# Block 2's norm and inverse by chunk halves, norms of blocks 3 and 4 queued behind queries, attention one step earlier

## Chip, core and metric

The kernel runs on one core of one Trainium2 chip. The metric is device time in microseconds (us). Before the change it is 1829.39 us (median of 3 runs, 1828.8 to 1829.55).

## What is computed

A gated linear recurrence over 768 steps for 4 sequences, 8 heads and 48 channels, and behind it a mixture of 8 experts whose gate is normalised over rows and columns eight times:

```
a = (a_re + i a_im) * min(|a|, 0.999) / (|a| + 1e-6)
S[t] = a[t] * S[t-1] + k[t] v[t]^T          # complex state, per head 48 x 48
y[t] = q[t] . Re S[t]
x = y as [3072, 384];  P = exp(x @ w_gate - max);  8 times: P /= row sums, P /= column sums, P *= 3072/8
out = sum over e of P[:, e] * (relu(x @ w1[e]) @ w2[e])     # w1: 384 x 1024, w2: 1024 x 384
```

## The kernel before, in words

The 3072 tokens are cut into 12 blocks of 256, each of two chunks of 128; a sequence has three blocks. Phase 1 works through the blocks; at the same time it runs experts 0 and 1 on the block before. Phase 2 runs the other six experts and the gate's iterations.

**Per block, VectorE and ScalarE** (`elem`, `chain`, L361 and L422). The decays `z` of the block are loaded. Then come the **norm** (L435 to L449: a square on ScalarE, a reciprocal root on ScalarE, two corrections, seven VectorE instructions that end with two products `z<-z,x`), the **scan** (L451: cumulative complex products inside each chunk of 128, some 45 small VectorE instructions), and the **inverse** (L457 to L472: square, reciprocal root and one correction, then the scaled keys `kh`, L470, and the queries `z<-z,qk`, L472). The names `sqs[i, n]` and `zl[i, n]` are the last ScalarE and the last VectorE instruction of the inverse of block i, half n. With `parts=None` each step is one instruction over both chunks (768 elements a partition); with `range(NCH)` it is one for each chunk (384). Before the change blocks 0 and 1 go by halves.

**Per block, attention** (`mix`, L475). Twelve DMAs on SyncE's queue (L495) move `kh` into `ks`, twelve on GpSimd's queue move `z` into `qs`, six for each chunk. Then TensorE transposes the keys (`ktp`, L516), forms scores (`sp`, L533) and state products (`U`, L526) and outputs (`y`, L550). VectorE masks the scores (`sc`, L536) and moves the state (L587 to L598). `mix` is a generator that is advanced ten times a block; the first advance issues keys and scores of chunk 0.

**Per block, experts** (`experts`, L176). Sixteen steps on the block before, two experts of eight slices. A step is nine matmuls into `ph` (L214), two ScalarE readings `hh` and `hf` (L226, L227), one VectorE difference `hl` (L228), and, three steps later, six matmuls into `po` (L187 to L189), the third of which needs `hl`. When an expert ends, `po` is copied to `yst` (L192) and stored to `ye_d` by SyncE's queue (L193).

**Order.** TensorE's order is written out by hand: step n of block i's loop, then one advance of `mix` if n is at least `LEAD[i]` (L330). What is left of `mix` after step 15 alternates with the last expert matmuls. The other engines' orders come from a scheduler that goes by priority (order of emission) on a simulated timeline; `issue_after(ins)` puts what a block of code emits behind `ins` on the engine of `ins`, and `add_manual_dep` does so for one pair. Each engine and each DMA queue then works strictly in its order. In block 1's loop the expert steps 7 to 9 are held behind instructions of the inverse of block 1 (`late`, L316).

Of the kernel before, what the change touches and what calls it, by code (L numbers as in the profile page):

```python
# [23 lines left out]
N1 = 8  # L24
RING = 12
LAG = 3
LEAD = {1: 12, 2: 11, 3: 10, 4: 7, 5: 5}
TR = 4
TB = 32
UN = 768  # L30
# [30 lines left out]
class Net:  # L61
# [9 lines left out]
    def build(self):  # L71
        tc, nc = self.tc, self.nc
        DR = bass.MemoryType.DRAM
        PS = bass.MemoryType.PSUM
        with ExitStack() as ctx:
            dram = ctx.enter_context(tc.tile_pool(name="dram", bufs=1, space=DR))
            cst = ctx.enter_context(tc.tile_pool(name="cst", bufs=1))
            self.wp = ctx.enter_context(tc.tile_pool(name="wp", bufs=RING))
            self.psA = ctx.enter_context(tc.tile_pool(name="psA", bufs=2, space=PS))

            self.ones = cst.tile([128, 128], F32, name="ones")
            nc.vector.memset(self.ones, 1.0)
            warm = cst.tile([128, 1], F32, name="warm")
            nc.scalar.activation(warm, self.ones[:, 0:1], AF.Abs_reciprocal_sqrt)
            self.ident = cst.tile([128, 128], F32, name="ident")
            nc.sync.dma_start(self.ident, self.idn)
            self.nident = cst.tile([128, 128], F32R, name="nident")
            nc.scalar.activation(self.nident, self.ident, AF.Copy, scale=-1.0)
            self.mask = cst.tile([128, 4, CH], U8, name="mask")
            tri = cst.tile([128, CH], F32, name="tri")  # L90
            nc.sync.dma_start(tri, self.msk)
            for j in range(4):
                nc.vector.tensor_copy(self.mask[:, j, :], tri)
            self.bm05 = cst.tile([128, 1], F32, name="bm05")
            nc.vector.memset(self.bm05, -0.5)
            self.wgs = cst.tile([128, NCT, 2 * E], F32R, name="wgs")
            self.two = cst.tile([2 * E, E], F32, name="two")
            nc.vector.tensor_tensor(self.two, self.ident[:2 * E, :E], self.ident[:2 * E, E:2 * E], ALU.add)
            wgr = cst.tile([128, NCT, E], F32, name="wgr")
            nc.sync.dma_start(wgr, self.wg)  # L100
            nc.scalar.activation(self.wgs[:, :, :E], wgr, AF.Copy)
            nc.vector.tensor_tensor(self.wgs[:, :, E:], wgr, self.wgs[:, :, :E].bitcast(F32), ALU.subtract)
            self.P = cst.tile([128, self.ntt, E], F32, name="P")

            ns = self.N // SUB
            self.fl = cst.tile([128, ns * (NCT * NCH + 2) + 4], F32, name="fl")
            self.ok = cst.tile([128, 9], F32, name="ok")
            self.oki = cst.tile([1, 1], mybir.dt.int32, name="oki")
            self.wt = {}
            self.x_d = [dram.tile([128, NS, 2, NCT, 2, CH], F32, name=f"x_d{u}") for u in range(self.N // UN)]  # L110
            self.ye_d = [[dram.tile([128, C], F32, name=f"ye_d{u}_{i}") for i in range(self.ntt)] for u in range(2)]
            self.dram = dram

            with ExitStack() as c2, tc.manual_schedule(engines={mybir.EngineType.PE}):
                with ExitStack() as c1:
                    with ExitStack() as ca:
                        self.phase1(c1, ca)
                    self.phase2a(c2)
                self.phase2b(c2)
            flag = nc.values_load(self.oki[0:1, 0:1], min_val=0, max_val=1)  # L120
            with tc.If(flag < 1):
                with ExitStack() as c3:
                    self.general(c3)
# [52 lines left out]
    def experts(self):  # L176
# [18 lines left out]
        while True:  # L195
            i, e, f = yield
            if i is None:
                for _ in range(len(pend) if e is None else min(e, len(pend))):
                    l2(*pend.pop(0))
                continue  # L200
            if len(pend) == LAG:
                l2(*pend.pop(0))
            xh, xl = self.xs[i]

            def group(f):
                w = self.wt[e, f]
                ph = self.psA.tile([128, SUB], F32, tag="ph", name=f"ph{e}_{i}_{f}")
                terms = [(ct, k, x) for ct in range(NCT) for k, x in ((0, xh), (0, xl), (1, xh))]
                if e == 0 and f < 2:
                    terms.sort(key=lambda t: t[2] is xl)  # L210
                for q, (ct, k, x) in enumerate(terms):
                    if x is xl and terms[q - 1][2] is xh:
                        yield ph
                    nc.tensor.matmul(ph, w[:, k, ct * 128:ct * 128 + 128], x[:, ct, :], start=q == 0, stop=q == len(terms) - 1)  # L214
                yield ph

            if e == 0 and f == 0:
                rest = [group(0), group(1)]
                for g in rest:
                    next(g)  # L220
            for ph in rest.pop(0) if rest else group(f):
                pass
            hh = self.hp.tile([128, SUB], F32R, tag="hh", name=f"hh{e}_{i}_{f}")
            hl = self.hp.tile([128, SUB], F32R, tag="hl", name=f"hl{e}_{i}_{f}")
            hf = self.hp.tile([128, SUB], F32, tag="hf", name=f"hf{e}_{i}_{f}", bufs=2)
            nc.scalar.activation(hh, ph, AF.Relu)  # L226
            self.hf = nc.scalar.activation(hf, ph, AF.Relu)  # L227
            nc.vector.tensor_tensor(hl, hf, hh.bitcast(F32), ALU.subtract)  # L228
            pend.append((i, e, f, hh, hl))

    def phase1(self, c1, ca):
# [27 lines left out]
        for t in self.rr + [self.sb]:  # L259
            nc.gpsimd.memset(t, 0.0)  # L260
        self.xs, self.vt, self.kqd, self.ql, self.sqs, self.zl, self.post = {}, {}, {}, {}, {}, {}, {}
        self.ev, self.dve, self.act, self.root, self.nthird = [], {}, {}, {}, 0
        ns = self.N // SUB
        self.moe = self.experts()
        next(self.moe)
# [13 lines left out]
        for i in range(ns):  # L279
# [33 lines left out]
            lg = self.logits(i - 1)  # L313
            if i == 1:
                q, z = [self.sqs[1, n] for n in range(NCH)], [self.zl[1, n] for n in range(NCH)]
                late = {7: (q[0], z[0]), 8: (q[1], z[0]), 9: (z[1],)}  # L316
            for n in range(2 * NF):
                with ExitStack() as st:
                    if i == 1 and n in late:
                        for ins in late[n]:  # L320
                            st.enter_context(tc.issue_after(ins.ins))
                    self.moe.send((i - 1, n // NF, n % NF))
# [11 lines left out]
                    self.moe.send((None, 1, None))  # L334
            if i + 1 < ns:
                self.elem(i + 1)
        lg = self.logits(ns - 1)
        for f in range(2):
            self.moe.send((ns - 1, 0, f))
# [21 lines left out]
    def elem(self, i, scratch=False):  # L361
# [17 lines left out]
        if not scratch:  # L379
# [5 lines left out]
                nc.sync.dma_start(qk, self.aqk[i, :, 2:4])  # L385
            nc.sync.dma_start(vt, self.v[i])

            self.chain(i, range(NCH) if i == 1 else None, zt, qk, alloc)
            return

        for n in range(NCH):
# [30 lines left out]
    def chain(self, i, parts, zt, qk, alloc):  # L422
# [3 lines left out]
        base = 2 * ns + ns * NCT * NCH  # L426
        z = zt[:, :, :, :CH]
        sq, x, y0, zz = alloc("sq"), alloc("x"), alloc("y0"), alloc("zz")
        for n in parts or [None]:
            f0, f1 = (base + i, base + 2 + i) if n else (i, ns + i)  # L430
            sq_, x_, y_, zz_, z_ = (t if n is None else half(t, n) for t in (sq, x, y0, zz, z))
            with ExitStack() as st:
                if i == 2:
                    st.enter_context(tc.issue_after(self.sqs[1, 1].ins))
                act = self.act[i, n or 0] = [nc.scalar.activation(sq_, z_, AF.Square, accum_out=fl[:, f0:f0 + 1])]  # L435
            ops = self.dve[i, f"n{n or 0}"] = []
            with ExitStack() as st:
                if i == 2:
                    st.enter_context(tc.issue_after(self.zl[1, 1].ins))
                ops.append(V.scalar_tensor_tensor(x_, sq_[:, 0], 1e-20, sq_[:, 1], ALU.max, ALU.add))  # L440
            act.append(nc.scalar.activation(y_, x_, AF.Abs_reciprocal_sqrt))
            act.append(nc.scalar.activation(zz_, y_, AF.Square, accum_out=fl[:, f1:f1 + 1]))
# [12 lines left out]
        for n in parts or [None]:  # L455
            sq_, x_, g_, z_, qk_, kh_ = (t if n is None else half(t, n) for t in (sq, x, g0, z, qk, kh))
            act = nc.scalar.activation(sq_, z_, AF.Square)  # L457
            self.post.setdefault(i, []).append(act)
            V.scalar_tensor_tensor(x_, sq_[:, 0], 1e-26, sq_[:, 1], ALU.max, ALU.add)
            o = 2 * ns + i * NCT * NCH + (n or 0) * NCT  # L460
            self.root[i, n or 0] = [nc.scalar.activation(g_, x_, AF.Abs_reciprocal_sqrt)]
            nc.scalar.activation(fl[:, o:o + x_.shape[1]], x_[:, :, CH - 1], AF.Copy)
# [172 lines left out]
    def check(self, sp, more=lambda k: None):  # L635
# [2 lines left out]
        t = sp.tile([128, max(P.shape[1], fl.shape[1])], F32, name="chk")  # L638
        for j, (src, thr, op) in enumerate((
                (fl[:, 0:ns], 2.0 ** 40, ALU.is_le), (fl[:, ns:2 * ns], 2.0 ** 18, ALU.is_le),  # L640
                (fl[:, 2 * ns:-4], 1e-24, ALU.is_ge), (fl[:, -4:-2], 2.0 ** 40, ALU.is_le), (fl[:, -2:], 2.0 ** 18, ALU.is_le), (P, 3e38, ALU.is_le), (P, -3e38, ALU.is_ge))):
            o = t[:, :src.shape[1]]
            nc.vector.tensor_scalar(o, src, thr, None, op)
            nc.vector.tensor_reduce(ok[:, j:j + 1], o, AX.X, ALU.min)
# [458 lines left out]
```

## Time and profile before

| | |
|---|---|
| median of 3 runs | 1829.39 us |
| profiled execution, its own time | 1823.66 us |
| its span | 1821.5 us |
| TensorE busy | 1764.9 us, 97% |
| VectorE busy | 1359.3 us, 75% |
| ScalarE busy | 729.3 us, 40% |
| mean granted TensorE clock | 0.994 |

Busy time is what the profiler recorded on an engine; idle time of TensorE is time in which its next matmul waited. The columns of the rows further down are named with them. Blocks are numbered from 0; the loop of block 2, which the change touches most, lies between 116 and 175 us, and phase 1 ends near 600 us.

### The profile page before, as it was taken

How to read it: one execution, taken by the hardware profiler on the slowest of the kernel's cores; microseconds unless marked ns; L12 is line 12 of the kernel's file. 1: busy time of each engine (PE TensorE's matmuls, PEld its weight loads, DVE VectorE, ACT ScalarE, POOL GpSimd, SP SyncE). 2: the span in 40 equal slices, each digit the busy share in tenths (PEclk: the TensorE clock that was granted, in tenths of full speed). 3: DMA queues.
4: the chain of work that ended last, by engine and by line, in shares of the span. 5: the costliest groups of instructions: out<-in, count | busy, mean ns of one | idle time of the engine just before them, and what ended most of it. 6: DMA issues, size and time to landing. Idle time of an engine off the chain costs nothing.

```text
span 1821.5 us, 30688 instructions
## 1 busy us (share of the span) xinstructions
PE 1764.9 (97%) x12024; PEld 1724.2 (95%) x12024; DVE 1359.3 (75%) x3023; ACT 729.3 (40%) x1597; POOL 89.2 (5%) x168
## 2 busy tenths in 40 slices
PE   6997999999999999999999999999999999999998
PEld 3896999999999999899999999999999999999998
DVE  8889899888873587867576757687776767675754
ACT  7453444544543433333242424243433334342421
POOL 4101111111110000000000000000000000000000
PEclk9998999999999999999999999999999999999999
DMA  7424344433332421401020101232220101020100
GB/s 222 117 82 126 90 120 116 131 106 111 116 99 97 133 87 41 134 14 56 1 70 1 53 18 53 70 104 70 87 70 18 53 18 53 2 69 1 53 27 28
DMA packets 104504, 132.83 MB, mean 73 GB/s; under 512 B 9632, under 2 KB 82080, under 8 KB 104352
## 3 DMA queue, kind: packets, MB, share of 16 engines
q1 hardware_dynamic: 98944, 120.89, 21.8%
q0 software_dynamic: 4608, 9.52, 2.1%
q8 instruction: 96, 1.57, 0.4%
q14 instruction: 56, 0.46, 0.1%
q10 hardware_dynamic: 800, 0.39, 0.1%
HBM read 88.22 MB, written 23.59 MB: 61 GB/s over the span
## 4 chain that ended last, share of the span: by engine, by line
PE 83%; DVE 11%; DMA 3%; ACT 1%; issue 1%; SPq 0%; DVEq 0%; ACTq 0%
PE po L828 10%; PE po L827 10%; PE po L826 10%; PE P L865 9%; PE P L867 9%; PE P L866 9%; PE ph L214 9%; PE po L187 3%; PE po L189 3%; PE po L188 3%; PE sp L533 2%; PE y L550 2%; DMA raw<-in_w_dram 1%; PE U L526 1%; PE ktp L516 1%
## 5 line engine op out<-in xcount | busy, mean ns | idle before, releaser
L828 PE MATMUL po<-wc,hl 128*128 128x384 f32 x1152 | 385.4, 335 | 2.8 <-DVE hl L887 2.8
L826 PE MATMUL po<-wc,hh 128*128 128x384 f32 x1152 | 385.0, 334 | 0.3 <-ACT hh L886 0.3
L827 PE MATMUL po<-wc,hh 128*128 128x384 f32 x1152 | 384.8, 334 | 0.0
L886 ACT ACTIVATE hh<-c 128x384 fp32r<-128x384 f32 x384 | 200.8, 524 | 322.6 <-DVE c L875 321.3
L887 DVE SCALAR_TENSOR_TENSOR hl<-c,hh 128x384 fp32r<-128x384 f32 x384 | 212.0, 552 | 65.8 <-ACT hh L886 58.0
L214 PE MATMUL ph<-xh,w 128*128 128x256 f32 x1152 | 226.9, 282 | 1.8 <-ACT xh L602 1.8
L828 PEld LDWEIGHTS po<-wc,hl 128*128 128x128 f32 x1152 | 216.2, 188 | 4.2 <-DVE hl L887 4.1
L826 PEld LDWEIGHTS po<-wc,hh 128*128 128x128 f32 x1152 | 216.3, 188 | 0.6 <-ACT hh L886 0.6
L827 PEld LDWEIGHTS po<-wc,hh 128*128 128x128 f32 x1152 | 216.3, 188 | 0.0
L880 ACT ACTIVATE s<-P 128x384 f32<-128x384 f32 x192 | 94.1, 490 | 274.3 <-PE P L867 274.2
L214 PEld LDWEIGHTS ph<-xh,w 128*128 128x128 f32 x1152 | 186.2, 190 | 2.8 <-ACT xh L602 2.6
L226 ACT ACTIVATE hh<-ph 128x256 fp32r<-128x256 f32 x192 | 73.2, 381 | 239.6 <-PE ph L214 239.1
L865 PE MATMUL P<-B,wa 128*128 128x384 f32 x480 | 160.5, 334 | 0.6 <-DVE c L875 0.6
L867 PE MATMUL P<-B,wa 128*128 128x384 f32 x480 | 160.4, 334 | 0.0
L866 PE MATMUL P<-B,wa 128*128 128x384 f32 x480 | 160.3, 334 | 0.0
L214 PE MATMUL ph<-xl,w 128*128 128x256 f32 x576 | 154.4, 282 | 1.4 <-DVE xl L603 1.4
L187 PE MATMUL po<-w,hh 128*128 128x384 f32 x384 | 140.5, 366 | 0.0
L189 PE MATMUL po<-w,hl 128*128 128x384 f32 x384 | 130.4, 340 | 3.6 <-DVE hl L228 3.6
L188 PE MATMUL po<-w,hh 128*128 128x384 f32 x384 | 129.7, 338 | 0.0
L875 DVE TENSOR_TENSOR c<-P,u 128x384 f32<-128x384 f32 x192 | 106.2, 553 | 31.2 <-PE P L867 30.1
L875 DVE TENSOR_TENSOR u<-u,s 128x384 f32<-128x384 f32 x96 | 53.4, 556 | 101.1 <-ACT s L880 100.8
L228 DVE TENSOR_TENSOR hl<-hf,hh 128x256 fp32r<-128x256 f32 x192 | 80.0, 419 | 48.3 <-ACT hf L227 46.4
(173 smaller groups left out, 3503.7 us busy)
## 6 DMA issues: line engine op xcount, KB each, us to landing
raw<-in_w_dram SPq DMA_DIRECT2D x48, 768.0 KB, 4.3
qs<-z POOLq DMA_DIRECT2D x144, 64.5 KB, 4.2
qk<-in_aqk_dram SPq DMA_DIRECT2D x12, 768.0 KB, 5.6
ks<-kh SPq DMA_DIRECT2D x144, 64.0 KB, 2.8
ye_d<-yst SPq DMA_DIRECT2D x48, 192.0 KB, 2.0
y<-ye_d SPq DMA_DIRECT2D x48, 192.0 KB, 2.4
z<-in_aqk_dram SPq DMA_DIRECT2D x11, 768.0 KB, 6.0
B<-x_d SPq DMA_DIRECT2D x40, 192.0 KB, 3.7
```

The source lines that it names most:

```text
L187: nc.tensor.matmul(po[k], hh[:, s], w2h, start=f == 0, stop=False)
L188: nc.tensor.matmul(po[k], hh[:, s], w2l, start=False, stop=False)
L189: nc.tensor.matmul(po[k], hl[:, s], w2h, start=False, stop=f == NF - 1)
L214: nc.tensor.matmul(ph, w[:, k, ct * 128:ct * 128 + 128], x[:, ct, :], start=q == 0, stop=q == len(terms) - 1)
L826: nc.tensor.matmul(po[k], hh[:, s], w2[:, 0, i], start=first, stop=False)
L827: nc.tensor.matmul(po[k], hh[:, s], w2[:, 1, i], start=False, stop=False)
L828: nc.tensor.matmul(po[k], hl[:, s], w2[:, 0, i], start=False, stop=last)
L865: nc.tensor.matmul(ps, t[:, 0, k], x[:, 0], start=first, stop=False)
L866: nc.tensor.matmul(ps, t[:, 0, k], x[:, 1], start=False, stop=False)
L867: nc.tensor.matmul(ps, t[:, 1, k], x[:, 0], start=False, stop=last)
L886: A.activation(hh, c, AF.Relu)
L887: V.scalar_tensor_tensor(hl, c, 0.0, hh.bitcast(F32), ALU.max, ALU.subtract)
```

## The change

Block 2 joins blocks 0 and 1 in doing norm and inverse by halves (`NHALF = 3`). Its VectorE and ScalarE orders are fixed by pairs: the two halves of the norm alternate, the first mask of block 1's scores stands behind the norm's fifth instruction, three expert readings and one key copy stand behind the norm's ScalarE instructions; in the inverse both squares come first, then half 0, then half 1. In block 1's loop the `hl` of expert steps 7 to 9 are held behind earlier instructions than before (L468 and L470 of half 0, in place of L472). In block 2's loop the readings of expert steps 5 to 7 are held behind the inverse's ScalarE instructions. The norms of blocks 3 and 4 are held behind the inverses of blocks 2 and 3, as block 2's norm already was behind block 1's. Attention of blocks 2 and 3 begins at steps 10 and 9 in place of 11 and 10. The flags' tile grows by two columns.

```diff
-LEAD = {1: 12, 2: 11, 3: 10, 4: 7, 5: 5}
+NHALF = 3
+LEAD = {1: 12, 2: 10, 3: 9, 4: 7, 5: 5}
...
-            nc.scalar.activation(hh, ph, AF.Relu)
+            self.hh[i, e * NF + f] = nc.scalar.activation(hh, ph, AF.Relu)
...
-                late = {7: (q[0], z[0]), 8: (q[1], z[0]), 9: (z[1],)}
+                x, k = self.dve[1, 0][2], self.dve[1, 0][4]
+                late = {7: (q[0], x), 8: (q[1], k), 9: (z[0],)}
+            if i == 2:
+                late = {5: (self.post[2][1],), 6: (self.sqs[2, 0],), 7: (self.sqs[2, 1],)}
...
-                    if i == 1 and n in late:
+                    if i in (1, 2) and n in late:
...
+            if i == 1:
+                n0, n1, p0, p1 = (self.dve[2, k] for k in ("n0", "n1", 0, 1))
+                pairs = [self.dve[2, "x0"] + self.dve[2, "x1"] + p0 + p1, self.post[2] + self.root[2, 0] + self.root[2, 1]]
+                pairs.append([t[k] for k in range(5) for t in (n0, n1)] + self.dve["m", NCH][:1] + n0[5:] + n1[5:])
+                a0, a1 = self.act[2, 0], self.act[2, 1]
+                pairs.append([t[k] for k in range(4) for t in (a0, a1)])
+                pairs += [[a1[k], self.hh[0, n]] for k, n in ((1, 12), (2, 13), (3, 14))] + [[a1[2], self.act["kt", 1, 0][0]]]
+                for order in pairs:
+                    for a, b in zip(order, order[1:]):
+                        tc.add_manual_dep(b.ins, a.ins.name, edge, reason="block 2 in order")
...
-            self.chain(i, range(NCH) if i == 1 else None, zt, qk, alloc)
+            self.chain(i, range(NCH) if i < NHALF else None, zt, qk, alloc)
...
+        prev = {2: (1, NCH - 1), 3: (2, NCH - 1), 4: (3, 0)}.get(i)
...
-                if i == 2:
-                    st.enter_context(tc.issue_after(self.sqs[1, 1].ins))
+                if prev:
+                    st.enter_context(tc.issue_after(self.sqs[prev].ins))
...
-                if i == 2:
-                    st.enter_context(tc.issue_after(self.zl[1, 1].ins))
+                if prev:
+                    st.enter_context(tc.issue_after(self.zl[prev].ins))
```

## Rows read from the trace of the kernel before

**Rows 1.** Windows: stretch, its length, busy us of each engine, TensorE clock, DMA.
```profile
150.00:200.00 50.00, 46.30 (x422) 43.73 (x422) 47.88 (x130) 21.48 (x55) 6.25 (x12) 0.97 0.50 132
250.00:300.00 50.00, 50.00 (x496) 47.98 (x496) 44.01 (x101) 25.43 (x63) 6.26 (x12) 1.00 0.36 107
```
**Rows 2.** Waits of TensorE, 100 to 182 us: total us, times, longest.
```profile
PE ktp L516 <- DMA ks<-kh: 4.4, 1, 4.4
PE sp L533 <- DMA qs<-z: 3.9, 1, 3.9
PE y L550 <- DVE sc L536: 1.6, 3, 0.8
PE ph L214 <- DVE xl L603: 1.4, 1, 1.4
PE ph L214 <- ACT xh L602: 1.2, 2, 0.6
```
**Rows 3.** Waits of all engines, 80 to 100 us.
```profile
PE po L189 <- DVE hl L228: 2.3, 1, 2.3
```
**Rows 4.** Windows behind the long waits.
```profile
84.62:88.20 3.58, 3.58 (x15) 3.58 (x16) 3.51 (x8) 1.51 (x4) 2.61 (x6) 0.54 0.79 200
144.14:145.15 1.01, 0.98 (x4) 0.63 (x4) 0.97 (x3) 0.00 (x0) 1.01 (x3) 0.50 0.78 193
149.00:153.20 4.20, 4.20 (x17) 4.20 (x18) 4.06 (x13) 0.00 (x0) 0.00 (x0) 0.51 0.79 228
```
**Rows 5.** Chain of waits, 76 to 96 us: start, us, engine, tile, line.
```profile
77.42 1.59 ACT sq L457 x2
...
92.42 0.39 PE ktp L516 x4
```
**Rows 6.** Chain of waits, 0 to 450 us.
```profile
136.59 1.07 PE ph L214 x9
...
199.55 0.91 PE sp L533 x8
...
243.79 0.91 PE sp L533 x8
```
**Rows 7.** Timeline of ScalarE at 126 us: start, us, instruction.
```profile
126.11 1.49 ACT L457 ACTIVATE sq<-z 128x1536 f32<-128x1536 f32 x1 [0.44 <-DVE z L359]
```
**Rows 8.** Timeline of VectorE: block 1's halves, then block 2 whole.
```profile
81.80 1.03 DVE L470 TENSOR_TENSOR kh<-x,z 128x384 f32<-128x384 f32 x2
82.74 1.02 DVE L472 TENSOR_TENSOR z<-z,qk 128x384 f32<-128x384 f32 x2
...
89.06 0.95 DVE L440 SCALAR_TENSOR_TENSOR x<-sq 128x768 f32<-128x768 f32 x1
...
98.56 1.83 DVE L449 TENSOR_TENSOR z<-z,x 128x768 f32<-128x768 f32 x2
...
137.59 1.81 DVE L470 TENSOR_TENSOR kh<-x,z 128x768 f32<-128x768 f32 x2
...
140.53 1.82 DVE L472 TENSOR_TENSOR z<-z,qk 128x768 f32<-128x768 f32 x2
```
**Rows 9.** Timeline of GpSimd, 55 to 300 us: the queries' DMA issues.
```profile
83.95 3.12 POOL L495 DMA_DIRECT2D qs<-z  x6 [27.04 <-ACT hh L226]
...
142.12 0.53 POOL L495 DMA_DIRECT2D qs<-z  x1 [50.94 <-ACT zz L445]
...
180.11 5.20 POOL L495 DMA_DIRECT2D qs<-z  x10 [31.43 <-ACT hf L227]
...
224.01 4.69 POOL L495 DMA_DIRECT2D qs<-z  x9 [36.84 <-DMA ks<-kh]
```
**Rows 10.** Timeline of SyncE's queue, 55 to 300 us.
```profile
136.65 0.81 SPq L193 DMA_DIRECT2D ye_d<-yst  x2
138.56 7.63 SPq L495 DMA_DIRECT2D ks<-kh  x12
```

More of the change, by code (lines that the diff above doesn't have):

```diff
@@ L105, in build @@
             ns = self.N // SUB
-            self.fl = cst.tile([128, ns * (NCT * NCH + 2) + 4], F32, name="fl")
+            self.fl = cst.tile([128, ns * (NCT * NCH + 2) + 2 * NHALF], F32, name="fl")
             self.ok = cst.tile([128, 9], F32, name="ok")
@@ L261, in phase1 @@
         self.xs, self.vt, self.kqd, self.ql, self.sqs, self.zl, self.post = {}, {}, {}, {}, {}, {}, {}
-        self.ev, self.dve, self.act, self.root, self.nthird = [], {}, {}, {}, 0
+        self.ev, self.dve, self.act, self.root, self.hh, self.nthird = [], {}, {}, {}, {}, 0
         ns = self.N // SUB
@@ L428, in chain @@
         sq, x, y0, zz = alloc("sq"), alloc("x"), alloc("y0"), alloc("zz")
+        prev = {2: (1, NCH - 1), 3: (2, NCH - 1), 4: (3, 0)}.get(i)
         for n in parts or [None]:
-            f0, f1 = (base + i, base + 2 + i) if n else (i, ns + i)
+            f0, f1 = (base + i, base + NHALF + i) if n else (i, ns + i)
             sq_, x_, y_, zz_, z_ = (t if n is None else half(t, n) for t in (sq, x, y0, zz, z))
             with ExitStack() as st:
-                if i == 2:
-                    st.enter_context(tc.issue_after(self.sqs[1, 1].ins))
+                if prev:
+                    st.enter_context(tc.issue_after(self.sqs[prev].ins))
                 act = self.act[i, n or 0] = [nc.scalar.activation(sq_, z_, AF.Square, accum_out=fl[:, f0:f0 + 1])]
@@ L458, in chain @@
             self.post.setdefault(i, []).append(act)
-            V.scalar_tensor_tensor(x_, sq_[:, 0], 1e-26, sq_[:, 1], ALU.max, ALU.add)
+            self.dve[i, f"x{n or 0}"] = [V.scalar_tensor_tensor(x_, sq_[:, 0], 1e-26, sq_[:, 1], ALU.max, ALU.add)]
             o = 2 * ns + i * NCT * NCH + (n or 0) * NCT
@@ L640, in check @@
                 (fl[:, 0:ns], 2.0 ** 40, ALU.is_le), (fl[:, ns:2 * ns], 2.0 ** 18, ALU.is_le),
-                (fl[:, 2 * ns:-4], 1e-24, ALU.is_ge), (fl[:, -4:-2], 2.0 ** 40, ALU.is_le), (fl[:, -2:], 2.0 ** 18, ALU.is_le), (P, 3e38, ALU.is_le), (P, -3e38, ALU.is_ge))):
+                (fl[:, 2 * ns:-2 * NHALF], 1e-24, ALU.is_ge), (fl[:, -2 * NHALF:-NHALF], 2.0 ** 40, ALU.is_le), (fl[:, -NHALF:], 2.0 ** 18, ALU.is_le), (P, 3e38, ALU.is_le), (P, -3e38, ALU.is_ge))):
             o = t[:, :src.shape[1]]
```

## Prediction

> **What bounds the kernel now.** I read the windows first. From 250 us on TensorE is busy in every microsecond of its stretch; between 150 and 200 us it is idle for 3.7 us of 50 [rows 1]. So what phase 1 loses, it loses early, and a microsecond won there reaches the end if nothing behind it takes it back. Second, TensorE's waits. In block 2's loop it stands still once for 4.4 us, for keys, and right behind that for 3.9 us, for queries [rows 2]; in block 1's loop once for 2.3 us, because `hl` of expert step 7 is late [rows 3]. Smaller waits at the ends of both loops sum to 1.6 + 1.4 + 1.2 = 4.2 us [rows 2]. [...] Fourth, why keys and queries are late: block 2's scan ends just before its square at 126.11 [rows 7], but its first key DMA goes out at 138.56 [rows 10] and its first query DMA at 142.12 [rows 9], as `kh` is written at 137.59 and the queries at 140.53 [rows 8].
>
> **The change, part by part.** Two spans carry the sum. In block 2 TensorE could go on 144.14 - 138.56 = 5.6 us after the first key DMA [rows 4, 10], and 149.00 - 142.12 = 6.9 us after the first query DMA [rows 4, 9]; both waits were ended by those DMAs [rows 2].
>
> *Inverse of block 2 by halves.* Block 1 shows the form: square at 77.42 [rows 5], `kh` of half 0 at 81.80 [rows 8], its first query DMA at 83.95 [rows 9]: 4.4 and 6.5 us. Block 2 whole took 137.59 - 126.11 = 11.5 and 16.0 us. I add 0.7 us for two `hl` that slip in (256 elements against 384 in 0.47 us [rows 8] are an estimated 0.31 each) and get 5.1 and 7.2 us: queries leave 8.8 us sooner after the scan.
>
> *Norm of block 2 by halves.* Whole, it ran from 89.06 to 98.56 + 1.83 = 100.39 [rows 8], 11.3 us for seven instructions of at most 0.95 us each, the last two of them 1.83 together, so some 6.6 us; the rest is VectorE idle or with `hl` while ScalarE works. Alternating halves fill those gaps: 6.6 us, plus an estimated 0.5 for halving, 0.5 for the pinned mask (512 elements), 0.7 for `hl`: 8.3 us, 3.0 us sooner. Below nothing it could lose about 1 us if the pinned mask waits for late scores. I take the scan's end at 126.1 - 3.0 = 123.1, and keep 126.1 for the range.
>
> *Price of halving.* Two half instructions 0.94 us apart from the next pair (81.80, 82.74) against 1.81 for a whole pair [rows 8] make 0.03 to 0.13 us per whole instruction, 0.5 to 2.2 us for 17; it is inside the figures above. [...]
>
> *Attention of block 2 one step earlier.* Step 10's matmuls end at 136.59 + 1.07 = 137.66 [rows 6]. Keys: `kh` at 123.1 + 5.1 = 128.2, its first DMA 0.6 us later, there at 134.4: no wait. Queries: 123.1 + 7.2 = 130.3, there at 137.2; scores are due at 137.66 + 0.39 [rows 5]: no wait. If the scan ends at 126.1 the queries come at 140.2 and TensorE waits 2.1 us. I take a remainder of 0.8 us. So 4.4 + 3.9 + 2.55 - 0.8 = 10.0 us are won (range 6.5 to 10.9).
>
> *Block 1's `hl`.* Held behind L468 and L470 in place of L472, step 7's `hl` comes before its need, and 2.3 + 1.65 = 3.95 us go. But then keys and scores of block 1 are due at 92.42 - 3.95 = 88.5 and 88.9, and the queries leave no sooner than 83.95, later by one or two `hl`: 84.4 + 6.9 = 91.3. [...] The wait moves and costs the same: I take 0 (from -1 to +3.95).
>
> *Ends of loops.* One advance more lies beside expert steps, one less among the last matmuls. I take 1.0 of the 4.2 us (from -1 to 2.9, the latter if block 2's end, now beside a scan, waits as little as block 1's).
>
> *Readings of steps 5 to 7 behind the inverse's ScalarE work, flags:* nothing. Squares and roots of half 0 are done by 126, about when those steps deliver; three steps lie between a reading and its use. If that cover is gone, one `hl` late costs what block 1's did.
>
> *Norms of 3 and 4 behind the queries.* They no longer interleave with the inverses, so ScalarE's legs show on VectorE, but queries of 3 come before norm 4. The question is what is late next: TensorE runs 10 us ahead. Block 3's scores, at 199.55 before, are due at 199.55 - 10 - 2.1 (one step) = 187.4; with the queries leaving at 180.11 as before they are there at 187.0. Block 4's are due at 243.79 - 10 = 233.8, there at 224.01 + 6.9 = 230.9 [rows 6, 9]. The margins are 0.4 and 2.9 us, before what VectorE gains from its earlier start. I charge 1.0 us (0 to 6).
>
> **Sum.** 10.0 + 0 + 1.0 - 1.0 = 10.0 us. The profiled execution took 1823.66 us, 5.7 under the median; it goes to 1813.7, and the median to 1829.4 - 10.0 = 1819.4.
>
> **Rivals.**
> 1. *VectorE takes part of it back.* For: it is busy 47.88 of 50 us in this stretch [rows 1] and the margins are thin. Against: from 250 us on it has 6 us of 50 free. A wait of 2 to 5 us for queries of block 2, 3 or 4, with up to 1.7 us of low clock, leaves 3.8 to 7: 1822.4 to 1825.6, say 1824.
> 2. *SyncE's queue holds the keys.* The store of `ye_d` at 136.65 stood before the keys [rows 10]. [...] Against: keys are ready 8 us before the store.
> 3. *More is won.* Queries of block 1 land sooner than bounded, the loop ends lose their waits: 3.5 us more, 1816.
> 4. *Slower: norms 3 and 4 put VectorE behind.* Lateness does not add over blocks, since TensorE's wait in one gives it back in the next; what counts is the slack before. Block 3's queries had 199.55 - 2.1 - 187.0 = 10.4 us, block 4's 243.79 - 230.9 = 12.9. Queries of block 4 later than that by any amount make the kernel slower. Serial legs on ScalarE (a square of 1536 elements at 1.49 [rows 7], two legs of 768 at an estimated 0.8) add 3.1 us each for norm 3, inverse 3 and norm 4, 9 in all if nothing fills them; with the scan not sooner and displaced attention work, 15: wait 2.1 us past the slack and 1.7 of low clock, 1833. Against: `hl` and masks fill such gaps.
>
> **How the numbers follow.** Forecast 0.50, rivals 1 to 4: 0.20, 0.12, 0.08, 0.10. About 0.2%, 3.7 us, is what a measurement can tell, so faster is under 1825.7. Forecast, rival 3 and most of rival 1 (0.17) are faster: 0.75. The rest of rival 1, all but a little of rival 2 make "same" 0.14, with rounding; slower 0.11. Range 1815.5 to 1827.0: it holds the first four cases' most.
>
> **What would show it.** Right: no wait over 1 us for `ks` or `qs` in block 2; clock 1.00 at 138 to 155 us; first query DMA of block 2 near 130; block 3's loop beginning near 165; a new wait on `qs` in block 1. Wrong: waits on `qs` in blocks 3 or 4, or the `ye_d` store ahead of block 2's first keys.

## The result, and the profile after

The changed kernel takes 1832.61 us (median of 20 runs, 1829.90 to 1837.86); the kernel before, run beside it, 1827.35 (20 runs, 1823.12 to 1829.55). The ratio is 1.0034, 95% interval 1.0026 to 1.0042: slower by some 5 to 6 us, where 10 us faster was forecast (from 1829.39, the median of the first 3 of those 20 runs). The profiled execution after took 1835.63 us, before 1823.66. Lines have moved down by 1 to 15 (`kh` is L485, `sp` L548, `hl` L229).

Windows of the profile after, cut where a loop begins (at the first gate matmul `lp<-xh`), the first window being the loop of block 1; columns as in [rows 1].

```profile
67.90:124.50 56.60, 51.98 (x466) 49.22 (x465) 50.16 (x146) 25.02 (x74) 6.26 (x12) 0.97 0.33 81
124.50:175.20 50.70, 48.02 (x436) 45.65 (x436) 43.74 (x108) 22.33 (x61) 6.27 (x12) 0.97 0.36 104
175.20:231.50 56.30, 50.96 (x429) 48.41 (x429) 47.02 (x106) 29.54 (x70) 6.24 (x12) 0.94 0.36 97
231.50:287.30 55.80, 50.13 (x454) 47.50 (x452) 53.20 (x115) 23.75 (x64) 10.94 (x21) 0.97 0.42 106
```

Before, the same loops began at 63.1, 117.9, 179.0, 229.0 and ended at 277.8 us (block 2's loop is 117.9 to 179.0, not 116 to 175 as said ahead):

```profile
63.10:117.90 54.80, 51.62 (x466) 49.13 (x464) 48.36 (x132) 24.51 (x68) 6.25 (x12) 0.97 0.33 85
117.90:179.00 61.10, 49.45 (x437) 46.51 (x436) 55.58 (x124) 28.79 (x67) 6.26 (x12) 0.92 0.34 95
179.00:229.00 50.00, 48.32 (x429) 45.80 (x427) 44.86 (x103) 23.61 (x62) 10.94 (x21) 1.00 0.41 103
229.00:277.80 48.80, 47.89 (x455) 45.79 (x453) 44.98 (x106) 23.07 (x61) 6.41 (x13) 1.00 0.43 125
```

Block 2's loop lost 10.4 us, as forecast; blocks 1, 3 and 4 took 1.8, 6.2 and 7.0 more. From block 5's loop on, each is as long as before within 0.1 us. So the four loops lose 4.7 us. The 12.0 us between the two profiled executions hold 4.8 us more from ahead of block 1's loop, which the diff does not touch, and 2.5 from the long rest of the span. These two executions lie far apart among their kernels' runs; in a second profile the loops repeat (below), the ends do not.

TensorE's waits after, to be held against [rows 2, 3]: first those between 80 and 124 us, then 100 to 182, then 182 to 290 (total us, times, longest).

```profile
PE ktp L531 <- DMA ks<-kh: 3.4, 1, 3.4
...
PE po L190 <- DVE hl L229: 1.8, 1, 1.8
PE ph L215 <- ACT xh L617: 1.4, 2, 0.7
...
PE y L565 <- DVE sc L551: 3.0, 3, 2.4
PE ktp L531 <- issue: 2.9, 1, 2.9
PE sp L548 <- DMA qs<-z: 2.6, 2, 2.2
PE po L190 <- DVE hl L229: 1.7, 1, 1.7
```

The 4.4 and 3.9 us of block 2 [rows 2] are gone. In block 1 the wait for `hl` [rows 3] has become one for keys, and between 182 and 290 us, where no single wait was over 0.9 us before, stand four kinds. ("issue" means that the profile shows nothing that the engine waited for.)

Why block 1's keys come late is in SyncE's queue after. Before, five key DMAs went out from 82.38 us, ahead of the store of `ye_d`; now three do, and since expert 0 no longer waits for `hl`, the store slips in earlier against them. The queue before, then after:

```profile
82.38 3.14 SPq L495 DMA_DIRECT2D ks<-kh  x5
85.66 1.29 SPq L193 DMA_DIRECT2D ye_d<-yst  x2
...
87.44 1.85 SPq L510 DMA_DIRECT2D ks<-kh  x3
89.50 0.90 SPq L194 DMA_DIRECT2D ye_d<-yst  x2
90.45 6.53 SPq L510 DMA_DIRECT2D ks<-kh  x9
```

Why blocks 3 and 4 are late is on VectorE. First the kernel before, 166 to 208 us: block 3's inverse begins (L459), **block 4's norm begins inside it** (L440), then come `kh` and queries of 3 (L470, L472), the norm's products (L449), and at 206.40, 22.6 us ahead of block 4's loop, the inverse of 4.

```profile
166.45 0.96 DVE L459 SCALAR_TENSOR_TENSOR x<-sq 128x768 f32<-128x768 f32 x1
169.89 0.96 DVE L440 SCALAR_TENSOR_TENSOR x<-sq 128x768 f32<-128x768 f32 x1 [0.56 <-ACT sq L435]
...
178.51 1.82 DVE L472 TENSOR_TENSOR z<-z,qk 128x768 f32<-128x768 f32 x2
181.79 1.82 DVE L449 TENSOR_TENSOR z<-z,x 128x768 f32<-128x768 f32 x2
...
206.40 0.96 DVE L459 SCALAR_TENSOR_TENSOR x<-sq 128x768 f32<-128x768 f32 x1 [2.51 <-ACT sq L457]
```

The same steps after: block 3's inverse begins 5.3 us **behind** the start of its loop (175.2), the norm of 4 (L455) follows the queries (L487), and the inverse of 4 begins only 6.8 us ahead of its loop.

```profile
180.53 0.96 DVE L474 SCALAR_TENSOR_TENSOR x<-sq 128x768 f32<-128x768 f32 x1 [1.22 <-ACT sq L472]
...
190.10 1.82 DVE L487 TENSOR_TENSOR z<-z,qk 128x768 f32<-128x768 f32 x2
191.84 0.95 DVE L455 SCALAR_TENSOR_TENSOR x<-sq 128x768 f32<-128x768 f32 x1
199.17 1.83 DVE L464 TENSOR_TENSOR z<-z,x 128x768 f32<-128x768 f32 x2
224.64 0.96 DVE L474 SCALAR_TENSOR_TENSOR x<-sq 128x768 f32<-128x768 f32 x1
```

Held apart, the two chains take 180.53 to 201.00 = 20.5 us; interleaved they took 166.45 to 183.61 = 17.2. In the experiments below, those with GpSimd left out, the pair took 16.8 to 20.5 us without the hold on block 4's norm, and 20.4 to 22.0 with it. And GpSimd's query issues for blocks 2, 3 and 4, to be held against 142.12, 180.11 and 224.01 [rows 9], are these:

```profile
140.11 0.53 POOL L510 DMA_DIRECT2D qs<-z  x1 [43.47 <-ACT hf L228]
...
191.70 6.24 POOL L510 DMA_DIRECT2D qs<-z  x12 [43.47 <-ACT hf L228]
241.23 6.24 POOL L510 DMA_DIRECT2D qs<-z  x12 [43.29 <-ACT hf L228]
```

### The profile page after: what moved, and what is told of

Same layout as the page of the kernel before. It is cut to its first block, busy times and chain, and to the rows that moved or that the text cites. A ratio compares the mean times of both kernels' runs of the same rounds, so it can differ in the third digit from the quotient of the medians.

```text
span 1833.5 us, 30712 instructions
## 1 busy us (share of the span) xinstructions
PE 1774.4 (97%) x12024; PEld 1731.9 (94%) x12024; DVE 1362.3 (74%) x3038; ACT 730.1 (40%) x1607; POOL 89.6 (5%) x168
## 4 chain that ended last, share of the span: by engine, by line
PE 80%; DVE 13%; DMA 4%; issue 2%; ACT 1%; SPq 1%; POOL 0%; DVEq 0%
PE po L843 10%; PE po L842 10%; PE po L841 10%; PE P L880 9%; PE P L882 9%; PE P L881 9%; PE ph L215 8%; PE po L188 3%; PE po L190 3%; PE po L189 3%; PE sp L548 2%; PE y L565 2%; DMA raw<-in_w_dram 1%; PE U L541 1%; DVE cm_a L368 1%
## 5 line engine op out<-in xcount | busy, mean ns | idle before, releaser
L229 DVE TENSOR_TENSOR hl<-hf,hh 128x256 fp32r<-128x256 f32 x192 | 80.0, 419 | 54.4 <-ACT hf L228 52.6
```

## The experiments

A norm is *held* here when it is queued behind the queries of the block before, as the change does for blocks 3 and 4. Each ratio is to the kernel before, run beside it on the same chip. "Start" is where block 1's loop begins, "loops" the lengths of the loops of blocks 1 to 4 in the profiled execution, "lead" the time from the start of a block's loop to the first VectorE instruction of its inverse (-6.8 is 6.8 us ahead of the loop, +5.3 is late). Where the text says that a lead falls, the inverse begins later against its loop.

| run | start | loops | lead of 3 | lead of 4 | ratio |
|---|---|---|---|---|---|
| before | 63.1 | 54.8, 61.1, 50.0, 48.8 | -12.6 | -22.6 | 1 |
| after | 67.9 | 56.6, 50.7, 56.2, 55.8 | +5.3 | -6.8 | 1.0034 [1.0026, 1.0042] |
| e1_noq | 63.0 | 57.6, 58.2, 49.1, 50.3 | -5.7 | -10.0 | 1.0001 [0.9992, 1.0009] |
| e2_onlyq | 63.6 | 54.9, 59.4, 49.5, 51.6 | -4.1 | -8.3 | 1.0018 [1.0007, 1.0029] |
| e3_oldlead | 68.0 | 56.9, 49.3, 57.4, 57.4 | +5.2 | -7.6 | 1.0046 [1.0029, 1.0063] |
| e4_oldlate | 63.0 | 55.0, 51.2, 56.2, 55.8 | +5.3 | -6.8 | 1.0010 [0.9998, 1.0022] |
| e5_again | 66.9 | 56.4, 50.7, 56.2, 55.8 | +5.3 | -6.8 | 1.0038 [1.0024, 1.0052] |
| e6_noq_oldlate | 67.2 | 55.1, 52.8, 53.7, 48.5 | -0.9 | -13.6 | 0.9976 [0.9958, 0.9993] |
| e9_light | 66.2 | 54.8, 48.7, 50.0, 57.0 | -0.9 | -6.8 | 0.9997 [0.9982, 1.0012] |
| e11_only3 | 66.8 | 56.8, 49.2, 61.3, 47.8 | +5.3 | -17.4 | 1.0009 [0.9999, 1.0020] |
| e12_only4 | 67.5 | 56.9, 54.5, 48.7, 57.5 | -5.0 | -6.8 | 1.0026 [1.0015, 1.0037] |
| e13_warm | 61.8 | 59.3, 48.7, 54.0, 55.5 | +0.2 | -7.2 | 1.0018 [1.0009, 1.0028] |
| e14_warm_e6 | 61.6 | 56.4, 49.2, 49.9, 50.3 | -2.6 | -10.0 | 0.9965 [0.9949, 0.9981] |
| e16_e6_oldlead | 63.2 | 55.0, 52.4, 58.6, 48.0 | +0.2 | -18.9 | 0.9993 [0.9978, 1.0009] |

**Norms 3 and 4 not held** (the rest of the change stays; "N" is the theory that the held norms make the loss, "L" that the earlier attention does).

```diff
-        prev = {2: (1, NCH - 1), 3: (2, NCH - 1), 4: (3, 0)}.get(i)
+        prev = {2: (1, NCH - 1)}.get(i)
```

> The changed kernel, but the norms of blocks 3 and 4 are not held behind the queries of blocks 2 and 3. Theory N (the held norms put VectorE behind, and blocks 3 and 4 lose for it): norm 4's products end near 188 us in place of 201, TensorE waits under 2 us in all for keys, queries and masks in the loops of blocks 3 and 4, and the ratio to the kernel before is 0.996 to 0.999. Rival L (attention one step earlier pushes the scan of block 3 back, whatever the norms do): norm 4 still ends near 200 us, ratio 1.002 to 1.005 as with the whole change.

Neither number: loops 3 and 4 came back to 49.1 and 50.3, but norm 4 ended at 193.6 us, and block 2's gain shrank from 10.4 to 2.9 us, since norm 3 now runs inside block 2's inverse. Against the changed kernel 0.0033, about 6 us, returned; the four loops hold 4.2 us of that, and this execution also started 4.9 us earlier.

**The held norms alone**, put into the kernel before.

```diff
+        prev = {2: (1, 1), 3: (2, 0), 4: (3, 0)}.get(i)
-                if i == 2:
-                    st.enter_context(tc.issue_after(self.sqs[1, 1].ins))
+                if prev:
+                    st.enter_context(tc.issue_after(self.sqs[prev].ins))
...
-                if i == 2:
-                    st.enter_context(tc.issue_after(self.zl[1, 1].ins))
+                if prev:
+                    st.enter_context(tc.issue_after(self.zl[prev].ins))
```

> The kernel before with the held norms of blocks 3 and 4 as the only edit. Theory N: norm 4's products end 6 to 17 us later than the 183.6 us of before; TensorE is not ahead here, so blocks 3 and 4 still have their 10 to 13 us of slack and most of it is used up: ratio 0.999 to 1.004, with a first wait for queries or masks in block 4's loop. Rival L: norm 4 ends within 4 us of before, no new wait, ratio 0.998 to 1.001.

Slower by itself: norm 4 ends at 194.1 us against 183.6. The four loops are only 0.7 us longer in all, block 5's loop 1.0.

**The attention back at steps 11 and 10.**

```diff
-LEAD = {1: 12, 2: 10, 3: 9, 4: 7, 5: 5}
+LEAD = {1: 12, 2: 11, 3: 10, 4: 7, 5: 5}
```

> The changed kernel with attention of blocks 2 and 3 back at steps 11 and 10. Theory N: the lateness of VectorE stays, TensorE only meets it a step later: ratio 1.001 to 1.004, norm 4's end within 4 us of 201. Rival L: the loss goes with the step, ratio 0.996 to 0.999, norm 4's end near 188 us.

N held, L fell: norm 4 still ends at 200.8, and loops 3 and 4 are no shorter.

**Block 1's steps 7 to 9 at their old places.**

```diff
-                late = {7: (q[0], x), 8: (q[1], k), 9: (z[0],)}
+                late = {7: (q[0], z[0]), 8: (q[1], z[0]), 9: (z[1],)}
```

> The changed kernel with the hl of expert steps 7 to 9 of block 1's loop held where they were before. Theory S (in block 1 the wait only moved, from hl to keys that stand behind the stores in SyncE's queue): the 3.4 us wait for keys goes, the wait of 2 to 2.5 us for hl comes back, ratio to the kernel before within 0.001 of that of the whole change (1.0024 to 1.0044). If the earlier hl had been worth its 3.95 us, the ratio would be 1.005 or more; if the stores' place costs more than it, 1.002 or less.

The wait for `hl` is back (2.35 us at 84.51), the one for keys is gone, and block 1's loop is 1.6 us shorter than after: what the change did there was a loss, and not the even exchange that theory S expected. The median gained more (0.0024) than the loops (1.2 us); this execution also started 4.9 us earlier.

**The changed kernel once more.** No edit.

> The changed kernel once more, nothing edited. Its first expert loop began at 67.9 us in its profiled execution, that of the kernel before at 63.1, on identical instruction orders up to there; two of the four experiments so far began at 63.0 to 63.6 with the change's other parts in them, and one at 68.0. Theory P (the later start belongs to this program): the loop begins at 67 to 69 us again, with TensorE at half clock between 47 and 57 us. Theory Q (it belongs to the execution): it begins near 63. In both the loops of blocks 3 and 4 take 56 us each (before: 50.0 and 48.8), and the ratio to the kernel before is 1.002 to 1.005.

The loops repeat to 0.2 us, and the start is late again, at 66.9.

**Without holds and without the moved steps of block 1**: the edits of e1_noq and e4_oldlate together.

> The changed kernel with two parts undone: the norms of blocks 3 and 4 are not held, and the attention of block 1 stands at its old steps; what is left is block 2 by chunk halves in fixed order, and block 2's attention one step earlier and behind its own queries. Theory T (VectorE has about 194 us of work in the 215 us of loops 1 to 4, and a wait removed in block 2 comes back later): loops 1 to 4 sum to 212 to 216 us, ratio 0.997 to 1.001, block 2's loop 50 to 56 us and one of blocks 3 and 4 at 52 or more. Rival S (the held norms alone took the gain, the rest is free): block 2's loop 51 us, blocks 3 and 4 at 49 to 50 each, sum 205 to 207, ratio 0.995 or less.

Faster than the kernel before. The sum of loops, 210.2 us, lies between the two ranges, 1.8 us under T's and 3.2 over S's; the ratio and loops 2 and 3 are as T says.

**Half of the `hl` on GpSimd**, in the kernel before and in the changed kernel with the old steps; the edit is the same.

```diff
-            nc.vector.tensor_tensor(hl, hf, hh.bitcast(F32), ALU.subtract)
+            (nc.gpsimd if i < 4 and f % 2 else nc.vector).tensor_tensor(hl, hf, hh.bitcast(F32), ALU.subtract)
```

> The kernel before with the subtraction of every second hidden tile (hl of odd f) of loops 1 to 4 on GpSimd in place of VectorE: 8 a loop, so some 32 x 0.34 = 11 us of VectorE's 194 us of work leave loops 1 to 4. Theory T (VectorE's throughput bounds these loops): loops 1 to 4 lose 4 to 11 us, ratio 0.994 to 0.998. Rival O (the waits come from the order and the latency of single steps, VectorE is not full): within 0.001 of the kernel before, or slower, because GpSimd's queue holds a hl behind query issues: then TensorE waits for hl on GpSimd.

> The changed kernel with the attention of block 1 at its old steps, and the same subtractions (odd f, loops 1 to 4) on GpSimd. Without the second edit the ratio was 1.001 and loops 3 and 4 took 56.2 and 55.8 us. Theory T: with 11 us less on VectorE loops 3 and 4 fall to 49 to 53 us, and the ratio to 0.990 to 0.997. Rival O: loops 3 and 4 stay at 55 us or more because the held norms' chain, not VectorE's load, sets them: ratio 1.000 or above.

Both slower: 1.0054 [1.0037, 1.0071] and 1.0045 [1.0028, 1.0061], loops 56.9, 60.0, 55.5, 50.3 and 61.4, 59.6, 52.8, 49.5. They are no clean test of T. Groups by line of the kernel before, then of the first of them, between 63 and 290 us (busy us, mean ns): 32 `hl` left VectorE, but its two-input products became slower, `kh` from 817 ns to 986, and its busy time in the four loops rose from 193.8 to 202.7 us. Part of that rise is more of the scan inside these loops: 57 products into `cm_b` where there were 50.

```profile
L470 DVE TENSOR_TENSOR kh<-x,z 128x768 f32<-128x768 f32 (+1 forms) x12 | 9.3, 817 | 0.1
...
L470 DVE TENSOR_TENSOR kh<-x,z 128x768 f32<-128x768 f32 (+1 forms) x12 | 11.4, 986 | 0.0
...
L228 POOL TENSOR_TENSOR hl<-hf,hh 128x256 fp32r<-128x256 f32 x32 | 39.1, 1225 | 127.7 <-ACT hf L227 101.8 <-DMA x_d<-xh 7.5 <-PE U L526 6.2
```

**Half of the `hl` not computed**, with zeros written by ScalarE, so that VectorE does have less to do; in the changed kernel, then in the kernel before.

```diff
-            nc.vector.tensor_tensor(hl, hf, hh.bitcast(F32), ALU.subtract)
+            if i < 4 and f % 2:
+                nc.scalar.activation(hl, hf, AF.Copy, scale=0.0)
+            else:
+                nc.vector.tensor_tensor(hl, hf, hh.bitcast(F32), ALU.subtract)
```

> The changed kernel, but in loops 1 to 4 the low half of every second hidden tile (hl of odd f) is not computed: ScalarE writes zeros there in place of VectorE's subtraction (this leaves out part of the precision). That is 8 x 4 x 0.42 = 13 us less on VectorE, without the load that GpSimd put on it (there VectorE's busy time in these loops rose from 193.8 to 202.7 us, and the loops from 214.7 to 222.7). Theory T (VectorE's work bounds loops 1 to 4): their sum falls from 219 to 204 to 211 us, loops 3 and 4 from 56 to 49 to 53 each, ratio to the kernel before 0.993 to 0.999. Rival O (the order set by the holds bounds loops 3 and 4, not the load): loops 3 and 4 keep 54 us or more each, ratio 1.002 or above.

> The kernel before with the same part left out (zeros from ScalarE for hl of odd f in loops 1 to 4). Theory T: the sum of loops 1 to 4 falls from 214.7 to 203 to 209 us, most of it in blocks 1 and 2, ratio 0.994 to 0.998. Rival O: the sum stays within 2 us, ratio within 0.0015 of 1.

T fell as a general bound. In the changed kernel the four loops are 8.8 us shorter in all: loop 3 came back to 50.0, as T says, but loop 4 stayed at 57.0, as O says; in the kernel before (start 63.9; loops 56.5, 59.0, 49.7, 48.0; ratio 0.9983 [0.9972, 0.9994]) 13 us less of `hl` on VectorE won 1.5 us of loops. (ScalarE's busy time in them rose by 10 us, which neither run separates.) Loop 4's one long wait in the first shows how lateness travels: ScalarE's square of block 5 waits for the scan on VectorE until 250.17 us, the reading `yst` stands behind it in ScalarE's order, and TensorE's next `po` waits 4.99 us for `yst` (timelines of ScalarE, then of TensorE).

```profile
250.17 1.48 ACT L475 ACTIVATE sq<-z 128x1536 f32<-128x1536 f32 x1 [3.54 <-DVE z L376]
251.56 0.85 ACT L193 ACTIVATE yst<-po 128x384 f32<-128x384 f32 x2
...
252.08 0.69 PE L188 MATMUL po<-w,hh 128*128 128x384 f32 x1 [4.99 <-ACT yst L193]
```

**One hold at a time**, in the changed kernel: only block 3's norm held, then only block 4's.

```diff
-        prev = {2: (1, NCH - 1), 3: (2, NCH - 1), 4: (3, 0)}.get(i)
+        prev = {2: (1, NCH - 1), 3: (2, NCH - 1)}.get(i)
```

```diff
-        prev = {2: (1, NCH - 1), 3: (2, NCH - 1), 4: (3, 0)}.get(i)
+        prev = {2: (1, NCH - 1), 4: (3, 0)}.get(i)
```

> The changed kernel with block 4's norm not held; block 3's still waits for block 2's second queries. If block 4's hold costs the loop of block 4 its 7 us, loop 4 is 49 to 51 us, loop 3 stays at 56, and the ratio is 0.999 to 1.001. If the loss comes from block 3's hold alone and is handed on, loop 4 stays at 54 us or more and the ratio at 1.002 or above.

> The changed kernel with block 3's norm not held; block 4's still waits for block 3's queries. If block 3's hold costs loop 3 its 6 us, loop 3 is 49 to 52 us and the ratio 0.999 to 1.001 with loop 4 at 52 or more. If the planner places block 3's norm between the halves of block 2's inverse, as in the kernel with neither norm held (there block 2's loop took 58.2 us), loop 2 is 56 us or more and the ratio 1.001 to 1.004.

This is the clearest pair. Windows of the loops of blocks 2, 3 and 4, first with block 3's norm held:

```profile
123.60:172.78 49.18, 46.53 (x437) 44.23 (x435) 43.71 (x108) 22.26 (x61) 6.27 (x12) 1.00 0.37 105
172.78:234.09 61.31, 51.92 (x428) 49.25 (x426) 55.11 (x117) 30.02 (x72) 10.29 (x20) 0.89 0.33 92
234.09:281.89 47.80, 47.65 (x454) 45.93 (x452) 44.42 (x104) 23.24 (x61) 7.28 (x14) 1.00 0.44 121
```

and with block 4's held:

```profile
124.38:178.92 54.54, 48.22 (x436) 45.69 (x434) 47.57 (x117) 25.64 (x65) 6.26 (x12) 0.97 0.32 88
178.92:227.61 48.69, 48.12 (x428) 45.79 (x426) 41.91 (x97) 25.77 (x66) 6.24 (x12) 1.00 0.44 118
227.61:285.08 57.47, 51.64 (x455) 48.91 (x452) 53.17 (x113) 23.81 (x64) 11.26 (x21) 0.94 0.43 111
```

A hold lengthens the loop of the block whose norm it holds: block 4's from 47.8 to 57.5 us, block 3's from 48.7 to 61.3, while block 3's hold shortens block 2's from 54.5 to 49.2. VectorE's busy time goes along (third figure behind the length: 44.4 against 53.2 in loop 4): the work that a hold puts off falls into the next loop. With block 4's hold taken away block 3's loop grows from 56.2 to 61.3, so its 8 us in block 4 are not all won. Taking it away returns 0.0025 of the changed kernel's 0.0034; taking block 3's away returns 0.0008, which the intervals do not tell from nothing.

**The start.** In 16 profiles without the edit below, TensorE's wait for block 0's keys and the start of block 1's loop go together: waits of 1.2 to 1.4 us and starts of 62.9 to 63.9 in eight, waits of 1.7 to 2.4 us and starts of 66.2 to 68.1 in the other eight. With the short wait the granted clock is low too, but for less long: 0.50 at 44 to 47 us and 0.98 at 47 to 57 in the profile before. Over 47 to 57 us it is 0.94 or more in the first eight and 0.58 or less in the others. The edit fills that wait with transposes of the identity, which the real ones overwrite: in the changed kernel, in e6_noq_oldlate, in the kernel before.

```diff
+                if i == 0 and c == 0 and g == 0:
+                    for j in range(16):
+                        nc.tensor.transpose(kt_p[:, j % 4, :], self.ident[:SK, :], self.ident[:SK, :SK])
                 for j in range(4):
                     nc.tensor.transpose(kt_p[:, j, :], ks[:, 4 * g + j, :], self.ident[:SK, :SK])
```

> The changed kernel with 16 transposes of the identity on TensorE (1.7 us at full clock) ahead of block 0's first keys, into the same PSUM tile, which the real transposes overwrite: they fill TensorE's wait for the keys there. Theory W (that wait lets the clock fall, and the 10 us at half clock cost 4 us): TensorE is at full clock between 47 and 57 us, the first loop begins at 63 to 64.5 us, and the ratio falls from 1.0034 to 1.001 to 1.002. Rival R (the late start has another cause, the weights' arrival): it begins at 66 or later, ratio 1.003 or above.

> The kernel with norms 3 and 4 not held and block 1's attention at its old steps (0.9976 of the kernel before, its first loop at 67.2 us in its profile), with the same 16 transposes. Theory W: start at 63 to 64.5 us and a ratio of 0.995 to 0.998, if the planner's orders in loops 1 to 4 stay as good (they sum to 210.2 us without the transposes; some of VectorE's order moves). Rival R: start at 66 or later, ratio 0.9975 or above.

> The kernel before with the same 16 transposes. Its own profile showed a wait of 1.2 us and a start at 63.1, so theory W expects a start at 63 to 64.5 us again, and a ratio of 0.998 to 1.0005: only executions in which the wait was longer gain. If the kernel before is late as often as the changed one, the ratio falls by as much as that of the changed kernel (0.0015 to 0.0025), and the late start is no part of the difference between the two.

W held. First the changed kernel: TensorE's timeline at the wait and the window behind it,

```profile
44.20 1.73 PE L531 MATMUL ktp<-ident,ks 112*128 112x112 f32 x8 [1.86 <-DMA ks<-kh]
...
47.00:57.00 10.00, 10.00 (x69) 8.81 (x68) 5.87 (x12) 1.92 (x6) 1.14 (x4) 0.50 0.84 221
```

then the same with the wait filled:

```profile
41.93 1.70 PE L532 MATMUL ktp<-ident 112*128 112x112 f32 x16
44.12 0.96 PE L534 MATMUL ktp<-ident,ks 112*128 112x112 f32 x8 [0.49 <-DMA ks<-kh]
...
47.00:57.00 10.00, 10.00 (x152) 9.23 (x154) 9.54 (x19) 4.52 (x14) 1.89 (x4) 1.00 0.81 220
```

The granted clock stays at 1.00 instead of 0.50, and 152 recorded matmuls pass in place of 69. The start falls from 67.9 to 61.8, the ratio from 1.0034 to 1.0018, some 3 us. In the kernel before the start is 63.9 and the ratio 0.9998 [0.9988, 1.0008]: nothing to win, and in all five profiles of it and of kernels built from it without the fill the wait is the short one. So up to half of the measured loss (0.0016 of 0.0034, each of the two uncertain by 0.001) may come from this clock, in a stage that the diff does not touch. Its share alone is not shown, as the fill shifts the loops too: the four are 1.8 us shorter than after in all, and in e14_warm_e6 4.3 us shorter than in e6_noq_oldlate.

**The attention of e6_noq_oldlate back at steps 11 and 10**: the edit of e3_oldlead.

> The kernel with norms 3 and 4 not held and block 1's attention at its old steps (ratio 0.9976; loops 1 to 4 sum to 210.2 us), with the attention of blocks 2 and 3 back at steps 11 and 10. If the earlier attention belongs to the gain, loop 2 is 53 to 58 us and the ratio 0.998 to 1.001; if the halves alone give it, the ratio stays at 0.996 to 0.998. With norms held, the old steps made the changed kernel no faster (1.0046 against 1.0034).

In between, and by the intervals unclear: loop 2 stays at 52.4, and loop 3 is longer (58.6 against 53.7). Without the holds the earlier attention seems to belong to the gain.

**The layout.** The kernel before with the tile of flags two columns wider, as the change makes it.

```diff
-            self.fl = cst.tile([128, ns * (NCT * NCH + 2) + 4], F32, name="fl")
+            fl = cst.tile([128, ns * (NCT * NCH + 2) + 6], F32, name="fl")
+            self.fl = fl[:, :ns * (NCT * NCH + 2) + 4]
```

> The kernel before with the flag tile (fl) two columns wider, as in the changed kernel; the two columns are not used, and every engine's order is the same. If the layout makes the late start, the first loop begins at 66 to 68 us in most executions and the ratio is 1.001 to 1.002. If not, it begins at 63 to 64 us and the ratio is within 0.001 of 1.

Start 62.9, loops 54.9, 61.1, 50.0, 48.8, ratio 1.0007 [0.9996, 1.0017]: no sign that the layout does it. Why the changed kernel's keys come late more often (8 of 11 profiles of kernels built from it without the fill, none of 5 built from the one before) stays open.

**The best version** is e14_warm_e6: block 2 by halves in fixed order, its attention at step 10, no holds on norms 3 and 4, block 1's steps as before, and the filled wait. It takes 1818.72 us (9 runs) beside 1826.05 for the kernel before. Its loops:

```profile
61.60:118.00 56.40, 51.95 (x466) 49.24 (x464) 52.30 (x152) 25.45 (x74) 6.27 (x12) 0.97 0.33 90
118.00:167.20 49.20, 46.58 (x436) 44.23 (x434) 44.10 (x111) 25.18 (x64) 6.27 (x12) 1.00 0.36 106
167.20:217.10 49.90, 48.39 (x428) 45.86 (x428) 44.72 (x100) 26.59 (x68) 6.35 (x12) 1.00 0.38 104
217.10:267.40 50.30, 47.94 (x454) 45.89 (x453) 47.92 (x107) 24.06 (x62) 8.85 (x17) 1.00 0.41 111
```

## Why the prediction was wrong

**The failed step is "Norms of 3 and 4 behind the queries", charged 1.0 us (0 to 6).** Loops 3 and 4 took 13.2 us more. The step took block 3's and 4's queries to leave "as before", at 180.11 and 224.01, with TensorE 10 us ahead of that. They left at 191.70 and 241.23, 6.8 and 12.4 us later even when the start's 4.8 us are taken off. Rival 4 named this mechanism, its place, and 1833 us, with a chance of 0.10; its deciding point of 12.9 us for block 4 was nearly met. But it spoke of queries that come late as a whole; what the loops show is dearer. Once a block's inverse begins close to its loop, the work that was ahead of the loop runs inside it: `ktp` and `sp` (2.9, 2.2 us) are late in block 3's loop, `hl` and a mask (1.7, 2.4) in block 4's, with a granted clock of 0.50 from 197.0 to 203.8. That its 1833 us came out is luck in part, as up to some 3 us belong to the start.

**The table shows where the length changes.** In the kernels in it, block 4's loop takes 47.8 to 51.6 us when its inverse begins 8.3 us or more ahead of the loop, and 55.5 to 57.5 when 7.6 or less. Block 3's takes 48.7 to 50.0 with 2.6 us or more, and 53.7 to 61.3 with less, but for the run with less VectorE work. That the hold moves the lead and the loop's length is shown by taking each hold away; that the lead is the only cause is not (the two runs with GpSimd have long leads and a loop 3 of 52.8 and 55.5).

**"A microsecond won there reaches the end if nothing behind it takes it back"** was the premise behind it. The lead of blocks 3 and 4 seems itself made by TensorE's long wait in block 2: while it stood, VectorE ran on. No run isolates that, but the table fits it. Without block 3's hold block 2's loop won 2.9, 8.3, 6.6, 11.9 and 8.7 us (e1, e6, e12, e14, e16), and block 3's lead fell by 6.9, 11.7, 7.6, 10.0 and 12.8; with the hold, 10.4 and 11.9 won (after, e11) took 17.9. In the kernels with neither hold the lead of block 4 falls from 22.6 us to between 10.0 and 18.9, and that can still be borne; where the change has block 4's hold as well it is 6.8 to 7.6, and is not. The prediction counted the margin to the queries alone, and not VectorE's other work in the loop.

**Block 2, 10.0 us: the size came out, 10.4 us, for another reason.** The scan's end is 0.5 us sooner after the start (not 3.0), the first query leaves 9.7 us behind it (not 7.2; an `hl` takes 0.42 us, not 0.31), and the hold that keeps norm 3 out of it is part of it: with block 3's hold alone the loop gains 11.9 us, with block 4's alone 6.6, with neither 2.9 (8.3 when block 1's steps are put back as well). So part of the 10 us was borrowed from block 3. The clock between 138 and 160 us was 1.00, and no wait for `ks` or `qs` is left there, as foreseen. The first query DMA left at 140.1 us, not near 130, and block 3's loop began at 175.2, not near 165 (its own 10 us make 169).

**The low clock, 2.55 us in block 2 (1.65 in block 1, 1.7 in the rivals).** No run shows these terms by themselves. They are the author's estimates from [rows 4]: half of 0.98 us and of 4.12 of the 4.20 us, and (1 - 0.54) x 3.58 us. What the runs showed is the clock: in block 2 it was 1.00 after (138 to 160 us), and between 47 and 57 us 69 matmuls were recorded at 0.50 (after) against 152 at 1.00 (e13_warm).

**Block 1's `hl`, 0 (-1 to 3.95): wrong by 1.6 to 1.8 us.** The wait did move, but to keys behind the `ye_d` store, the mechanism that rival 2 saw for block 2. **Ends of loops, +1.0:** the waits of masks, `xl` and `xh` there fell from 4.2 to 1.4 us. But `hl` now waits 1.8 us at 128.66, and the clock behind it is low for 3.4 us (0.50 in this window), half of which, an estimated 1.7 us, is lost; about nothing is left.

```profile
128.73:132.13 3.40, 3.40 (x13) 3.18 (x14) 3.12 (x9) 1.88 (x3) 0.00 (x0) 0.50 0.00 0
```

**The start** was in no term: no edit touches it, and up to some 3 us came on top. No run undoes the halves or the fixed orders of block 2 by themselves, so what they win or cost alone is not shown.

## What to carry to other kernels

A wait that is removed may also have fed someone (block 3's lead fell by 6.9 to 17.9 us here): before its microseconds are counted, measure how early each later block's chain starts against the loop that needs it, and expect the gain to be taken from those leads. Two chains that each wait for another engine were cheaper interleaved here (16.8 to 20.5 us) than one behind the other (20.4 to 22.0); a hold that gives one of them priority puts the other's work into the next loop (VectorE 53.2 us busy in block 4's, against 44.4). And where TensorE waits at a place that cannot be mended, a few idle transposes (16 here, 1.70 us) can be worth more than the wait, as in the changed kernel (a wait of 1.86 us; block 1's loop starts at 61.8 in place of 67.9), or nothing, as in the kernel before (63.9 beside 63.1).

## Not expected of the hardware

- A wait of 1.7 to 2.4 us between stretches of matmuls was followed by a granted clock of 0.50 to 0.58 over 47 to 57 us, and one of 1.2 to 1.4 us by a clock of 0.94 or more there, eight profiles each; block 1's loop starts some 4 us later in the first. Whether the execution or the kernel decides which comes is open; the changed kernel was late in both of its profiles.
- GpSimd took 1225 ns for a subtraction that takes VectorE 419, a single one 3.74 us (its spans are rough). Beside it VectorE's products of two SBUF tensors took longer: `kh` 986 against 817 ns, the queries 906 against 817, the norm's 1008 against 953. The `hl` left on VectorE, which also have two SBUF inputs, kept their time (417 against 419 ns). No run shows what makes the products slower.
